# Attention into channel mix on one core: softmax weights turned by VectorE and DMAs in place of TensorE from the third batch on

## The chip, the cores and the metric

One core of a Trainium2 chip runs the whole program. The metric is the time of one execution in microseconds (us). The kernel before has a median of 829.65 us over 3 runs (829.41 to 830.24).

## The reference

q, k and v have 8 batches of 8 heads, 576 positions and 64 dimensions; s has one number for each head and position. Everything is float32. The output of the attention, with the heads side by side, is the input x of the second half.

```
scores = q @ k.T / 8                           # per batch and head, 576 x 576
cum    = cumsum(max(s, 0))
scores = where(key > query, -1e9, scores + min(-(cum[query] - cum[key]), 0))
attn   = exp(scores - rowmax);  attn = attn / (rowsum + 1e-9)
x      = attn @ v                              # (8, 576, 512)

xk = mu_k * x + (1 - mu_k) * x_prev            # x_prev: x one position earlier
xr = mu_r * x + (1 - mu_r) * x_prev
k  = max(xk @ w_k, 0)                          # 512 -> 1024
out = sigmoid(xr @ w_r) * ((k * k) @ w_v)      # 1024 -> 512
```

## The kernel before

**Visits and chunks.** A visit is one batch and one pair of heads. The first batch is visited in two parts for each pair (8 short visits), the other seven batches whole (28 visits), so there are 36 visits. The channel mix goes over 18 chunks of 256 tokens; a batch has 2.25 of them. A chunk can start once all four visits of its batch have stored their output to x_d in DRAM.

**One head of a whole visit.** The queries lie in five tiles t = 0 to 4 of 64, 128, 128, 128 and 128 rows, the keys in five blocks kb of 128, 128, 128, 128 and 64. `products` (L816) makes the scores of a query tile against all keys up to its end, as two matmuls in TensorE's reduced fp32 form (high and low halves); VectorE takes them out of PSUM with the row's minimum (L833); ScalarE exponentiates in place (L851); GpSimd divides by the row sum (L868, `normalize`). The result W has queries on partitions. The product with v needs keys on partitions. `weighted` therefore turns W by matmuls against an identity: 10 blocks of 128x128 (L933, `turn`) and 2 that hold two 64-column remainders together (L948, `turn_half`) for each head; ScalarE copies the turned blocks from PSUM to `ph` in seven pieces (L974, L991, L1003). So that two remainders lie side by side, VectorE writes the last 64 columns of tiles 2 and 4 in front of the rest (`lead`), in an instruction of its own, and tile 0's normalized weights go behind tile 1's. `both_heads` (L907) then makes the product with v for both heads at once, each head in its own 64 columns of the array, with full fp32 matmuls (each recorded as two instructions): per visit six products of 128, 448, 448, 320, 192 and 64 columns, 1600 in all. ScalarE copies the sums to xT (L1044), a DMA stores xT (L1350).

**Inputs.** For visits after the first batch a DMA brings k and q (raw, L747), GpSimd splits them in two (L769, L773), and four SBUF to SBUF DMAs of 64 partitions and 288 KB each place the halves (L782).

**Order.** All instructions are tasks of a planner (`Plan`). It puts them in a fixed order for each engine by a list schedule with written-out costs, due times and 40 passes forward and back; the order with the shortest planned time is emitted. Each engine, and the SP queue that issues nearly all DMAs, then works in that order and waits where a task isn't ready. The planner's costs for the new steps: a VectorE turn n/0.96 + 68 ns for n columns, a DMA 520 ns of the queue and 1300 ns more until it has landed.

Of the kernel before, what the change touches and what calls it, by code (L numbers as in the profile page):

```python
# [12 lines left out]
F32 = mybir.dt.float32  # L13
# [324 lines left out]
def forgetting_attention_then_channel_mix(  # L338
# [46 lines left out]
    def fixed(t):  # L385
        b = Buffer(lambda: t)
        b.ap = t
        return b
# [106 lines left out]


    NH = col(NQ - 1, P * (NQ - 1)) + 64
    phs = [fixed(const.tile([P, NH], F32, name=f"ph{j}")) for j in range(2)]

    def zero(t):  # L500
        for kb in range(NQ):
# [36 lines left out]
        )  # L538

    def constant_rows():  # L540
        for x in KLs + G2s:
            pool(lambda x=x: nc.gpsimd.memset(f32(x.get()[64:P]), 0.0), [], [(x, 1)], 2 * S, 36)
        for x in G2s:
            pool(
                lambda x=x: nc.gpsimd.memset(f32(x.get()[64 : 64 + PIECES]), 1.0), [], [(x, 1)], 2 * S, 36
            )
# [203 lines left out]
    def split_qk(x, b, hp):  # L750

        n = S
        KH = sbuf([P, 2, n], "KH", 2, F32R)
        G = sbuf([P, 2, n], "G", 2, F32R)
        KL, G2 = KLs[turns[0] % 2], G2s[turns[0] % 2]
        turns[0] += 1
        row = b * H + 2 * hp
        dma(
            lambda: nc.sync.dma_start(
                f32(KL.get()[64 : 64 + PIECES]), cum_d.ap[row : row + 2].rearrange("h p t -> p h t")  # L760
            ),
            [cum_d, (KL, 1)], [(KL, (j, 2)) for j in range(2)], 520,
        )

        def halves(r):
            return [(j, r) for j in range(2)]

        pool(
            lambda: nc.gpsimd.tensor_copy(KH.get(), x.get()),  # L769
            [(x, 0)], [(KH, p) for p in halves(0) + halves(1)], 2 * n, 114,  # L770
        )
        pool(
            lambda: nc.gpsimd.tensor_tensor(  # L773
                out=G.get(), in0=x.get(), in1=f32(KH.get()), op=ALU.subtract
            ),
            [(x, 0)] + [(KH, p) for p in halves(0) + halves(1)], [(G, p) for p in halves(0) + halves(1)],
            2 * n, 114, 2.21,
        )

        def move(to, a, y, c, r0, r1):  # L780
            dma(
                lambda: nc.sync.dma_start(f32(to.get()[a : a + 64]), f32(y.get()[c : c + 64])),  # L782
                [(y, p) for p in halves(r1)], [(to, p) for p in halves(r0)], 1370,
            )

        move(KL, 0, G, 0, 0, 0)
        move(G2, 0, KH, 64, 0, 1)
        move(G, 0, KH, 64, 0, 1)
        move(KH, 64, KH, 0, 1, 0)
        return G, G2, KH, KL  # L790

    def scores(b, h, tiles, G, G2, KH, KL):

        nm, sums, rinv = (sbuf([P, n], x, 2) for x, n in (("nm", 3 * NQ), ("sums", NQ), ("rinv", NQ)))
        if 0 in tiles:
# [4 lines left out]
        def products(t, m, i, k0, w, W):  # L800
            ps = bank(1, "s", 2)
            q0 = QS[t] - QS[tiles[0]]
            if G2 is None:
                pe(
                    lambda: nc.tensor.matmul(
                        ps.get()[:, :w],
                        G.get()[0:65, h % 2, q0 : q0 + P],
                        KH.get()[0:65, h % 2, k0 : k0 + w],
                        start=True,
                        stop=True,  # L810
                    ),
                    [(y, (h % 2, r)) for y in (G, KH) for r in range(2)], [ps], w, P, 4 / 2.4,
                )
            for x, (g, K) in enumerate(((G, KH), (G2, KL)) if G2 is not None else ()):
                pe(
                    lambda x=x, g=g, K=K: nc.tensor.matmul(  # L816
                        ps.get()[:m, :w],
                        g.get()[:, h % 2, q0 : q0 + m],
                        K.get()[:, h % 2, k0 : k0 + w],
                        start=x == 0,  # L820
                        stop=x == 1,
                    ),
                    [(g, (h % 2, 0)), (K, (h % 2, 0))]
                    + ([(g, 1), (K, (h % 2, 2))] if x else [(g, (h % 2, 1)), (K, (h % 2, 1))]), [ps], w, m,
                )

            n = KN[t]
            for a, e in ((k0, min(k0 + w, n - lead(t))), (max(k0, n - lead(t)), k0 + w)):
                if a >= e:
                    continue  # L830
                at = a + lead(t) if a < n - lead(t) else 0
                dve(
                    lambda a=a, e=e, at=at, i=i: nc.vector.tensor_tensor_reduce(  # L833
                        out=W.ap[:m, at : at + e - a],
                        in0=ps.get()[:m, a - k0 : e - k0],
                        in1=causal.get()[:m, S - P - QS[t] + a : S - P - QS[t] + e],
                        scale=-SCALE,
                        scalar=3.0e38 if i == 0 else nm.get()[:m, 3 * t + i - 1 : 3 * t + i],
                        op0=ALU.add,
                        op1=ALU.min,  # L840
                        accum_out=nm.get()[:m, 3 * t + i : 3 * t + i + 1],
                    ),
                    [ps, causal] + ([(nm, (t, i - 1))] if i else []),
                    [(W, i), (nm, (t, i))], e - a, ports="PS>S",
                )
                i += 1
            return i
# [12 lines left out]
            )  # L860

        def normalize(t, m, n, W):
            def to():
                u, a = pt[1].at
                return piece(u, a + P, 64, F32)[:64] if t == 0 else W.ap[:m, :n]

            pool(
                lambda: nc.gpsimd.tensor_scalar(  # L868
                    out=to(),
                    in0=W.ap[:m, :n],  # L870
                    scalar1=rinv.get()[:m, t : t + 1],
                    scalar2=1.0,
                    op0=ALU.mult,
                    op1=ALU.mult,
                ),
                [rinv] + [(pt[x], i) for x in (t, 1)[: 1 + (t == 0)] for i in range(3)],
                [(pt[1], 3)] if t == 0 else [(W, i) for i in range(3)], n, 244,
            )

        def rs(x):  # L880
            return x.get()[:, tiles[0] : tiles[-1] + 1]
# [13 lines left out]
        dve(lambda: nc.vector.reciprocal(rs(rinv), rs(rinv)), [], [rinv], 8 * len(tiles))  # L895
        for t in sorted(tiles, key=lambda t: t or 1.5):
            normalize(t, QN[t], KN[t], pt[t])
        return pt

    SWITCH = 95.0 + 54.0  # L900
# [19 lines left out]
        )  # L920
        plan.columns[i] = 4 * n

    def weighted(pts, V, xT, tiles):


        def transposed(pt, ph):
# [96 lines left out]
            if len(tiles) == NQ:  # L1023
                turned((0,))
                turned([(1, 2), (3, 4)], (2,))
                return turned((1,), (3,))
            elif tiles[0] == 0:
                turned((0,), [(1, 2)], (1,))
            else:
                turned((0, 2))  # L1030
                turned([(3, 4)], (2,), (3,))
        rest = [transposed(pt, ph) for pt, ph in zip(pts, phs)][1]
        po = bank(1, "po", 1)
        (*_, (q0, q1)) = spans = sums_of(tiles)
# [7 lines left out]
        for (a, e), ps in zip(spans, (rest, po)[-len(spans) :]):  # L1042
            act(
                lambda a=a, e=e, ps=ps: nc.scalar.copy(xT.get()[:, 1 + a : 1 + e], ps.get()[:, 0 : e - a]),  # L1044
                [ps], [(xT, a)], e - a, ports="P>S",
            )

    def sums_of(tiles):

# [226 lines left out]
    visits += [(b, hp, ALL) for b in range(1, B) for hp in range(NP)]  # L1276

    PLAIN = 8
    HEAD = 11200.0
    CHUNK = 40600.0  # L1280
    MARGIN = 25000.0
# [47 lines left out]
    prefix_sums()  # L1329
    plan.due = 25000.0  # L1330
    constant_rows()
    plan.due = 1000.0
    load_mu()
    for o in range(DF // 512):
# [7 lines left out]
    def finish(pts, V, xT, n, due):  # L1342
        b, hp, tiles = visits[n]
        plan.due = due
        weighted(pts, V, xT, tiles)
        q0, q1 = QS[tiles[0]], QS[tiles[-1]] + QN[tiles[-1]]

        c = slice(1 + q0 if q0 else 0, 1 + q1)
        dma(
            lambda: nc.sync.dma_start(x_d[b].ap[:, hp, c], xT.get()[:, c]),  # L1350
            [(xT, -1)] + [(xT, x) for x, _ in sums_of(tiles)],
            [(x_d[b], (hp, y)) for y in range(2) if tiles is ALL or y == (q0 > 0)],
            1300 * (q1 - q0) / S,
        )
        if hp == NP - 1:
            there[b] = q1

    for n, (b, hp, tiles) in enumerate(visits):
# [3 lines left out]
        if 0 < n < len(visits) - 1:  # L1362
            load(n + 1)
        plan.due = due
        xT = sbuf([P, S + 1], "xT", 2)
        pool(lambda xT=xT: nc.gpsimd.memset(xT.get()[:, 0:1], 0.0), [], [(xT, -1)], 2, 36)
        for j in range(2):
            plan.due = due + j * step
            pt = scores(b, 2 * hp + j, tiles, *QKs[n])
            if j == 0:  # L1370
                other = pt
            else:
                finish((other, pt), Vs[n], xT, n, due + (j + WDUE) * step)
            if j == 0 and n + 1 < len(visits):
                plan.due = due + SPLIT * step
                prepare(n + 1)
# [54 lines left out]
```

## Time and profile before

| | |
|---|---|
| median of 3 runs | 829.65 us |
| the profiled execution: its time, its span | 832.11 us, 830.3 us |
| TensorE busy, share of the span | 814.3 us, 98% |
| VectorE, ScalarE, GpSimd busy | 482.8, 558.5, 348.8 us |
| DMA moved | 104.9 MB, mean 126 GB/s |
| granted TensorE clock, mean | 0.99 |

Busy time is what the profile records as running; for TensorE it covers overlapping records, so a busy TensorE can still be waiting in parts. The span runs from the first to the last instruction; the 1.8 us beside it lie around the program.

### The profile page before, as it was taken

How to read it: one execution, taken by the hardware profiler on the slowest of the kernel's cores; microseconds unless marked ns; L12 is line 12 of the kernel's file. 1: busy time of each engine (PE TensorE's matmuls, PEld its weight loads, DVE VectorE, ACT ScalarE, POOL GpSimd, SP SyncE). 2: the span in 40 equal slices, each digit the busy share in tenths (PEclk: the TensorE clock that was granted, in tenths of full speed). 3: DMA queues.
4: the chain of work that ended last, by engine and by line, in shares of the span. 5: the costliest groups of instructions: out<-in, count | busy, mean ns of one | idle time of the engine just before them, and what ended most of it. 6: DMA issues, size and time to landing. Idle time of an engine off the chain costs nothing.

```text
span 830.3 us, 16178 instructions
## 1 busy us (share of the span) xinstructions
PE 814.3 (98%) x5498; PEld 686.1 (83%) x5498; DVE 482.8 (58%) x1628; ACT 558.5 (67%) x1641; POOL 348.8 (42%) x620
## 2 busy tenths in 40 slices
PE   8989899999999999999999999999999999999998
PEld 5568689788888879887988888888888787988997
DVE  6999858376455655475554645465645655436421
ACT  4887679687586866688585867577757767546421
POOL 8996876453444345343343433434443332100000
PEclk8999899999999999999999999999999999999999
DMA  7878658645544455444634453555354341012000
GB/s 220 254 243 260 156 158 207 170 126 143 138 121 124 117 142 114 132 128 127 168 103 118 110 157 99 136 134 153 95 131 115 97 119 37 28 47 64 14 26 25
DMA packets 47266, 104.90 MB, mean 126 GB/s; under 512 B 7518, under 2 KB 21092, under 8 KB 47184
## 3 DMA queue, kind: packets, MB, share of 16 engines
q1 hardware_dynamic: 47024, 103.71, 46.1%
q8 instruction: 43, 0.70, 0.4%
q14 instruction: 39, 0.32, 0.1%
q10 hardware_dynamic: 160, 0.16, 0.1%
HBM read 51.34 MB, written 19.48 MB: 85 GB/s over the span
## 4 chain that ended last, share of the span: by engine, by line
PE 77%; ACT 8%; POOL 5%; DVE 5%; DMA 3%; issue 2%; POOLq 0%; ACTq 0%
PE m L1220 19%; PE m L1148 17%; PE s L816 9%; PE m L1190 9%; PE po L907 8%; PE t L933 5%; ACT xp L1085 3%; DMA x<-x_d 3%; ACT W L851 2%; DVE xp L1096 2%; PE s L1220 2%; POOL W L868 2%; PE s L1148 1%; PE t L1148 1%; PE t L1220 1%
## 5 line engine op out<-in xcount | busy, mean ns | idle before, releaser
L851 ACT ACTIVATE W<-W,nm 128x448 f32<-128x448 f32 (+4 forms) x320 | 179.3, 562 | 73.0 <-DVE nm L833 66.1
L833 DVE CUSTOM_DVE_ANT_0 W<-s,causal 64x64 f32<-64x64 f32 (+4 forms) x320 | 129.2, 412 | 127.2 <-PE s L816 104.2
L1148 PE MATMUL m<-xh,w_k 128*128 128x256 f32 x1024 | 201.5, 285 | 0.0
L868 POOL TENSOR_SCALAR W<-W,rinv 128x448 f32<-128x448 f32 (+4 forms) x320 | 164.9, 536 | 19.7 <-DVE rinv L895 16.9
L1220 PE MATMUL m<-w_v,kh 128*128 128x512 f32 (+1 forms) x512 | 171.0, 394 | 0.0
L1148 PEld LDWEIGHTS m<-xh,w_k 128*128 128x128 f32 x1024 | 164.2, 189 | 1.4
L1148 PE MATMUL m<-xl,w_k 128*128 128x256 f32 x512 | 144.7, 283 | 0.0
L974 ACT COPY ph<-t 128x256 f32<-128x256 f32 (+3 forms) x264 | 102.1, 420 | 14.6 <-PE t L933 13.7
L1220 PEld LDWEIGHTS m<-w_v,kh 128*128 128x128 f32 x512 | 94.6, 188 | 15.2
L1096 DVE SCALAR_TENSOR_TENSOR xp<-x,mu,xp 128x256 f32<-128x256 f32 (+3 forms) x172 | 72.0, 419 | 51.6 <-ACT xp L1085 48.9
L1220 PE MATMUL m<-w_v,kl 128*128 128x512 f32 (+1 forms) x256 | 101.5, 397 | 0.0
L816 PE MATMUL s<-KH,G 128*64 128x64 f32 x336 | 97.3, 299 | 4.1 <-DVE nm L833 4.1
L890 POOL TENSOR_SCALAR rinv<-sums 128x5 f32<-128x5 f32 (+2 forms) x72 | 17.2, 240 | 194.5 <-ACT W L851 191.0
L1148 PEld LDWEIGHTS m<-xl,w_k 128*128 128x128 f32 x512 | 97.1, 190 | 0.8
L816 PE MATMUL s<-KL,G 128*64 128x64 f32 x336 | 97.0, 297 | 0.0
L907 PE MATMUL po<-ph,V 128*64 128x448 f32 (+4 forms) x688 | 94.5, 407 | 0.0
L1085 ACT ACTIVATE xp<-x,mu 128x256 f32<-128x256 f32 (+3 forms) x172 | 72.4, 421 | 29.1 <-DMA x<-x_d 9.6
L933 PE MATMUL t<-ident_r,Wr 128*128 128x128 f32 x640 | 87.9, 250 | 3.5 <-POOL W L868 2.4
L1190 PE MATMUL m<-w_r,xh 128*128 128x512 f32 x256 | 88.7, 403 | 0.9 <-DVE kl L1177 0.8
L933 PEld LDWEIGHTS t<-ident_r,Wr 128*128 128x128 f32 x640 | 68.7, 141 | 13.8 <-POOL W L868 5.8
L773 POOL TENSOR_TENSOR G<-raw,KH 128x1152 fp32r<-128x1152 f32 x28 | 74.9, 2676 | 1.9
L907 PEld LDWEIGHTS po<-ph,V 128*64 128x64 f32 x688 | 45.9, 139 | 33.1 <-issue 19.8
(130 smaller groups left out, 1356.9 us busy)
## 6 DMA issues: line engine op xcount, KB each, us to landing
raw<-in_q SPq DMA_DIRECT2D x28, 576.0 KB
G<-KH SPq DMA_DIRECT2D x56, 288.0 KB
V<-in_v SPq DMA_DIRECT2D x32, 320.0 KB
out<-g SPq DMA_DIRECT2D x35, 256.0 KB
x_d<-xT SPq DMA_DIRECT2D x28, 288.5 KB
KL<-G SPq DMA_DIRECT2D x28, 288.0 KB
KH<-KH SPq DMA_DIRECT2D x28, 288.0 KB
x<-x_d SPq DMA_DIRECT2D x12, 514.0 KB
```

The source lines that it names most:

```text
L816: lambda x=x, g=g, K=K: nc.tensor.matmul(ps.get()[:m, :w], g.get()[:, h % 2, q0 : q0 + m], K.get()[:, h % 2, k0 : k0 + w], start=x == 0, s ...
L833: lambda a=a, e=e, at=at, i=i: nc.vector.tensor_tensor_reduce(out=W.ap[:m, at : at + e - a], in0=ps.get()[:m, a - k0 : e - k0], in1=causal ...
L851: lambda: nc.scalar.activation(W.ap[:m, :n], W.ap[:m, :n], AF.Exp, bias=nm.get()[:m, 3 * t + mi : 3 * t + mi + 1], scale=-1.0, accum_out=s ...
L868: lambda: nc.gpsimd.tensor_scalar(out=to(), in0=W.ap[:m, :n], scalar1=rinv.get()[:m, t : t + 1], scalar2=1.0, op0=ALU.mult, op1=ALU.mult,),
L907: nc.tensor.matmul(po.get()[64 * j : 64 * j + 64, at : at + n], V.get()[:, kb, j], phs[j].get()[:, col(kb, a) : col(kb, a) + n], start=fir ...
L933: lambda: nc.tensor.transpose(ps.get()[0:m, place : place + P].bitcast(F32R), piece(pt[t].at[0], pt[t].at[1] + lead(t) + k0, m), ident_r.ap,),
L974: act(lambda: nc.scalar.copy(strips(ph), src()), [ps], [(ph, k) for k in ks], n * m, ports="P>S")
L1085: lambda n=n, o=o, i=i, to=to: nc.scalar.activation(to(), x.get()[:, c, o + i + 1 : o + i + 1 + n], AF.Copy, scale=mu.ap[:, which, c : c + 1],
L1096: lambda n=n, o=o, i=i, to=to: nc.vector.scalar_tensor_tensor(out=to(), in0=x.get()[:, c, o + i : o + i + n], scalar=mu1.ap[:, which, c : ...
L1148: lambda u=u, f=f, c=c, n=n, w=w, x=x: nc.tensor.matmul(ps.get()[:, u * CT : (u + 1) * CT], weight["k", c, f // 4].get()[:, w, f % 4 * P : ...
L1190: lambda c=c, n=n, x=x, w=w: nc.tensor.matmul(ps.get(), x.get()[:, c, ts], weight["r", c, 0].get()[:, w], start=c == 0 and n == 0, stop=c ...
L1220: lambda f=f, n=n, x=x, w=w, ps=ps, ms=ms: nc.tensor.matmul(ps.get()[:, :m], x.get()[:, f, ts], weight["v", f, 0].get()[:, w, ms], start=f ...
```

## The change

For visits 12 to 35 (`n >= BLOCKS`), which are batches 2 to 7, both heads' weights are turned otherwise. VectorE transposes W in blocks of 32x32 inside each group of 32 partitions and writes them to a new tile `turned` (`turn_blocks`): nine instructions for a head, with 64 to 512 columns, 1600 columns in all. When both heads are there, 16 DMAs move one quarter of the partitions each (32 partitions, 3840 bytes a partition) to a new tile `across`, which takes the place of both `ph` tiles; key group i of each DMA becomes a stretch of columns, so that keys lie on partitions. The product with v has nine products for a visit, of 64, 512, 64, 384, 64, 256, 64, 128 and 64 columns, again 1600. Visits 0 to 11 keep TensorE's transposes.

With it: `turned` and `across` have one buffer each; xT has one buffer in place of two, for all visits. Tiles 2 and 4 of the new visits are no longer written in two pieces (`first` is 0). Tile 0 is normalized in place. The second score matmul (`x` = 1) reads 67 partitions in place of 128, so that the four memsets of its unused rows and the wait on them go; four memsets (`blanks`) zero the parts of `turned` that no transpose writes. Planned costs, due times and steps are otherwise the same, and the planner orders everything anew.

```
...
+    ph_both = const.tile([P, 2 * NH], F32, name="ph")
+    phs = [fixed(ph_both[:, j * NH : (j + 1) * NH]) for j in range(2)]
+    NS = NQ * (NQ + 1)
+    turned_d = fixed(const.tile([P, 4, NS, 32], F32, name="turned"))
+    across = fixed(ph_both[:, 0 : 4 * NS * 32].rearrange("p (i s x) -> p i s x", i=4, s=NS))
+    across.last = phs
+    def slots(h, kb, t):
+        return (NQ + 1) * kb + t + 1 if h == 0 else (NQ + 1) * t + kb
+    def blanks():
...
-        for x in KLs + G2s:
-            pool(lambda x=x: nc.gpsimd.memset(f32(x.get()[64:P]), 0.0), [], [(x, 1)], 2 * S, 36)
...
-            [cum_d, (KL, 1)], [(KL, (j, 2)) for j in range(2)], 520,
+            [cum_d], [(KL, (j, 2)) for j in range(2)], 520,
...
-                        g.get()[:, h % 2, q0 : q0 + m],
-                        K.get()[:, h % 2, k0 : k0 + w],
+                        g.get()[: 64 + PIECES if x else P, h % 2, q0 : q0 + m],
+                        K.get()[: 64 + PIECES if x else P, h % 2, k0 : k0 + w],
...
-            n = KN[t]
+            n, first = KN[t], 0 if blocks else lead(t)
...
+        def turn_blocks(t, m, W):
+            j = h % 2
+            def at(a, e, g):
+                step = slots(j, 1, t) - slots(j, 0, t)
+                k0 = slots(j, a, t)
+                return turned_d.get()[:m, 0:g, k0 : k0 + step * (e - a - 1) + 1 : step].rearrange("p g k x -> p k g x")
+            for a, e, g in ((0, t, 4), (t, t + 1, 2)):
+                if a == e:
+                    continue
+                n = (e - a) * 32 * g
+                dve(
+                    lambda a=a, e=e, g=g, n=n: nc.vector.transpose(
+                        at(a, e, g),
+                        W.ap[:m, P * a : P * a + n].rearrange("p (k g x) -> p k g x", g=g, x=32),
+                    ),
+                    [(W, i) for i in range(3)], [(turned_d, (j, t))], n, ports="S>S",
+                )
...
+    def weighted_across(V, xT):
+        for g in range(4):
+            for i in range(4):
+                dma(
+                    lambda g=g, i=i: nc.sync.dma_start(
+                        across.get()[32 * g : 32 * g + 32, i], turned_d.get()[32 * i : 32 * i + 32, g]
+                    ),
+                    [(turned_d, (h, t)) for h in range(2) for t in range(NQ)], [(across, (g, i))], 520,
+                )
+        po, rest = bank(1, "po", 1), bank(1, "t", 2)
+        todo = [(rest, 0, 0, 0, 0, 2)]
+        for kb in range(NQ):
+            if kb:
+                todo.append((po, kb - 1, kb, kb, 2, 4))
+            if kb < NQ - 1:
+                todo.append((po, kb, kb, kb + 1, 0, 4))
...
+    BLOCKS = 12
...
-        xT = sbuf([P, S + 1], "xT", 2)
+        xT = sbuf([P, S + 1], "xT", 1)
```

## Rows read from the trace of the kernel before

**Rows 1.** The page: busy time by engine; the last chain, by engine.
```profile
PE 814.3 (98%) x5498; PEld 686.1 (83%) x5498; DVE 482.8 (58%) x1628; ACT 558.5 (67%) x1641; POOL 348.8 (42%) x620
...
PE 77%; ACT 8%; POOL 5%; DVE 5%; DMA 3%; issue 2%; POOLq 0%; ACTq 0%
```

**Rows 2.** SP's issues in time; L1350's issues after 190 us; start, duration.
```profile
194.28 0.83 SPq L1350 DMA_DIRECT2D x_d<-xT  x1
729.74 0.32 SPq L1350 DMA_DIRECT2D x_d<-xT  x1
...
L1350 SPq DMA_DIRECT2D x_d<-xT x24: 319/332/1164, 194.3 to 729.7; - x24
```

**Rows 3.** Busy time by stretch: stretch, length, engines, PEclk, DMA share, GB/s.
```profile
0.00:100.00 100.00, 90.06 (x563) 66.12 (x565) 89.34 (x273) 72.02 (x224) 83.29 (x150) 0.92 0.79 231
194.30:729.70 535.40, 532.46 (x3667) 453.19 (x3666) 293.97 (x1047) 374.41 (x1103) 207.87 (x373) 1.00 0.45 118
729.70:830.30 100.60, 97.50 (x587) 86.44 (x585) 40.92 (x76) 35.71 (x74) 0.00 (x0) 1.00 0.11 36
```

**Rows 4.** TensorE and its weight loads in time around eight transposes.
```profile
433.44 0.46 PE L933 MATMUL t<-ident_r,Wr 128*128 128x128 f32 x4
434.08 0.46 PE L1220 MATMUL m<-w_v,kh 128*128 128x512 f32 x1
...
433.21 0.55 PEld L933 LDWEIGHTS t<-ident_r,Wr 128*128 128x128 f32 x4
434.04 0.19 PEld L1220 LDWEIGHTS m<-w_v,kh 128*128 128x128 f32 x1
```

**Rows 5.** TensorE in time at one visit's product with v; L907 by form.
```profile
438.82 0.97 PE L907 MATMUL po<-ph,V 128*64 128x448 f32 x4
439.62 0.39 PE L907 MATMUL t<-ph,V 128*64 128x128 f32 x4
439.84 1.90 PE L907 MATMUL po<-ph,V 128*64 128x448 f32 x16
441.67 0.24 PE L816 MATMUL s<-KH,G 128*64 128x64 f32 x1
...
L907 PE MATMUL po<-ph,V 128*64 128x448 f32 x184 | 43.6, 552 | 0.0
L907 PE MATMUL po<-ph,V 128*64 128x64 f32 x92 | 6.5, 220 | 0.0
```

**Rows 6.** Four stretches around DMAs: columns as in rows 3.
```profile
401.80:403.30 1.50, 1.50 (x8) 1.21 (x7) 0.00 (x0) 0.00 (x0) 1.50 (x1) 1.00 0.87 184
427.75:429.25 1.50, 1.50 (x8) 1.20 (x7) 0.00 (x0) 1.46 (x7) 1.50 (x1) 1.00 0.87 189
430.50:435.20 4.70, 4.70 (x27) 3.98 (x26) 3.10 (x12) 4.64 (x16) 2.58 (x5) 1.00 0.94 250
```

**Rows 7.** L782's issues: ns least, median, most.
```profile
L782 SPq DMA_DIRECT2D KL<-G x28: 461/467/621, 69.6 to 665.8; - x28
```

**Rows 8.** VectorE groups by form: busy us, mean ns | idle before; two instructions in time.
```profile
L1119 DVE TENSOR_TENSOR xl<-xp,xh 128x512 fp32r<-128x512 f32 x64 | 44.0, 688 | 21.0 <-ACT xh L1115 20.7
L833 DVE CUSTOM_DVE_ANT_0 W<-s,causal,nm 128x64 f32<-128x64 f32 x128 | 35.7, 279 | 1.9
L833 DVE DVE_READ_ACCUMULATOR2_ANT nm<- 128x1 f32 x448 | 37.0, 83 | 0.0
...
430.44 0.32 DVE L833 CUSTOM_DVE_ANT_0 W<-s,causal 128x192 f32<-128x192 f32 x1
430.68 0.42 DVE L833 CUSTOM_DVE_ANT_0 W<-s,causal 128x256 f32<-128x256 f32 x1
```

**Rows 9.** ScalarE's copies of turned blocks, two of six forms.
```profile
L974 ACT COPY ph<-t 128x512 f32<-128x512 f32 x64 | 37.5, 586 | 7.4 <-PE t L933 7.2
L1003 ACT COPY ph<-t 64x128 f32<-64x128 f32 x112 | 29.5, 263 | 0.8
```

**Rows 10.** The last head's reciprocal; five normalizing instructions of one head.
```profile
715.54 0.19 DVE L895 RECIPROCAL rinv<-rinv 128x5 f32<-128x5 f32 x1 [0.59 <-POOL rinv L890]
...
439.85 2.57 POOL L868 TENSOR_SCALAR W<-W,rinv 128x192 f32<-128x192 f32 x5 [0.34 <-DVE rinv L895]
```

**Rows 11.** Waits: who for whom, us, times, longest.
```profile
POOL xT L1366 <- DMA x_d<-xT: 44.1, 10, 9.8
```

More of the change, by code (lines that the diff above doesn't have):

```diff
@@ L497, in forgetting_attention_then_channel_mix @@
     NH = col(NQ - 1, P * (NQ - 1)) + 64
-    phs = [fixed(const.tile([P, NH], F32, name=f"ph{j}")) for j in range(2)]
+    ph_both = const.tile([P, 2 * NH], F32, name="ph")
[7 more added lines that the diff above has]
+    def blanks():
+        u = turned_d.get()
+        for h in range(2):
+            a, step = slots(h, 0, 0), slots(h, 1, 1) - slots(h, 0, 0)
+            pool(
+                lambda a=a, step=step: nc.gpsimd.memset(
+                    u[:, 2:4, a : a + step * (NQ - 1) + 1 : step], 0.0
+                ),
+                [], [(turned_d, (h, t)) for t in range(NQ)], 64 * NQ, 36,
+            )
+            pool(
+                lambda a=a: nc.gpsimd.memset(u[64:P, 0:2, a : a + 1], 0.0), [], [(turned_d, (h, 0))], 64, 36,
+            )
     def zero(t):
@@ L790, in split_qk, with scores @@
         return G, G2, KH, KL
-    def scores(b, h, tiles, G, G2, KH, KL):
+    def scores(b, h, tiles, blocks, G, G2, KH, KL):
         nm, sums, rinv = (sbuf([P, n], x, 2) for x, n in (("nm", 3 * NQ), ("sums", NQ), ("rinv", NQ)))
@@ L825, in products @@
                 )
-            n = KN[t]
-            for a, e in ((k0, min(k0 + w, n - lead(t))), (max(k0, n - lead(t)), k0 + w)):
+            n, first = KN[t], 0 if blocks else lead(t)
+            for a, e in ((k0, min(k0 + w, n - first)), (max(k0, n - first), k0 + w)):
                 if a >= e:
                     continue
-                at = a + lead(t) if a < n - lead(t) else 0
+                at = a + first if a < n - first else 0
                 dve(
@@ L862, in normalize @@
         def normalize(t, m, n, W):
+            aside = t == 0 and not blocks
             def to():
                 u, a = pt[1].at
-                return piece(u, a + P, 64, F32)[:64] if t == 0 else W.ap[:m, :n]
+                return piece(u, a + P, 64, F32)[:64] if aside else W.ap[:m, :n]
             pool(
@@ L875, in normalize @@
                 ),
-                [rinv] + [(pt[x], i) for x in (t, 1)[: 1 + (t == 0)] for i in range(3)],
-                [(pt[1], 3)] if t == 0 else [(W, i) for i in range(3)], n, 244,
-            )
+                [rinv] + [(pt[x], i) for x in (t, 1)[: 1 + aside] for i in range(3)],
+                [(pt[1], 3)] if aside else [(W, i) for i in range(3)], n, 244,
+            )
+        def turn_blocks(t, m, W):
[14 more added lines that the diff above has]
+                    [(W, i) for i in range(3)], [(turned_d, (j, t))], n, ports="S>S",
+                )
         def rs(x):
@@ L897, in scores @@
             normalize(t, QN[t], KN[t], pt[t])
+            if blocks:
+                turn_blocks(t, QN[t], pt[t])
         return pt
@@ L921, in both_heads, with weighted @@
         plan.columns[i] = 4 * n
-    def weighted(pts, V, xT, tiles):
+    def weighted(pts, V, xT, tiles, blocks):
         def transposed(pt, ph):
@@ L1031, in transposed @@
                 turned([(3, 4)], (2,), (3,))
+        if blocks:
+            return weighted_across(V, xT)
         rest = [transposed(pt, ph) for pt, ph in zip(pts, phs)][1]
@@ L1046, in weighted, with columns, emit @@
             )
+    def weighted_across(V, xT):
[4 more added lines that the diff above has]
+                        across.get()[32 * g : 32 * g + 32, i], turned_d.get()[32 * i : 32 * i + 32, g]
+                    ),
+                    [(turned_d, (h, t)) for h in range(2) for t in range(NQ)], [(across, (g, i))], 520,
+                )
+        po, rest = bank(1, "po", 1), bank(1, "t", 2)
[5 more added lines that the diff above has]
+                todo.append((po, kb, kb, kb + 1, 0, 4))
+        def columns(h, kb, t, i, e):
+            n = 1 if e - i == 2 else NQ - t
+            step = slots(h, kb, 1) - slots(h, kb, 0)
+            a = slots(h, kb, t)
+            return across.get()[:, i:e, a : a + step * (n - 1) + 1 : step], n
+        def emit():
+            for ps, at, kb, t, i, e in todo:
+                for j in range(2):
+                    x, n = columns(j, kb, t, i, e)
+                    to = ps.get()[64 * j : 64 * j + 64]
+                    if ps is po:
+                        to = to.rearrange("p (i t x) -> p i t x", i=4, t=NQ - 1)[:, i:e, at : at + n]
+                    else:
+                        to = to[:, 0:64].rearrange("p (i t x) -> p i t x", i=2, t=1)
+                    nc.tensor.matmul(
+                        to, V.get()[:, kb, j], x,
+                        start=ps is rest or kb == 0, stop=ps is rest or kb == NQ - 1 or t == NQ - 1,
+                        skip_group_check=True,
+                    )
+        n = sum((e - i) * 32 * (1 if e - i == 2 else NQ - t) for _, _, _, t, i, e in todo)
+        k = plan.add(
+            "PE", SWITCH + 107.0 + n * 4 / 2.4, emit,
+            [V] + [(across, (g, i)) for g in range(4) for i in range(4)], [rest, po], land=54.0,
+        )
+        plan.columns[k] = 4 * n
+        act(
+            lambda: nc.scalar.copy(xT.get()[:, 1 : 1 + 64], rest.get()[:, 0:64]), [rest], [(xT, 0)], 64, ports="P>S",
+        )
+        act(
+            lambda: nc.scalar.copy(
+                xT.get()[:, 1 + 64 : 1 + S].rearrange("p (t i x) -> p i t x", t=NQ - 1, i=4),
+                po.get().rearrange("p (i t x) -> p i t x", i=4, t=NQ - 1),
+            ),
+            [po], [(xT, P)], S - 64, ports="P>S",
+        )
@@ L1331, in forgetting_attention_then_channel_mix @@
     constant_rows()
+    plan.due = 50000.0
+    blanks()
     plan.due = 1000.0
@@ L1344, in finish @@
         plan.due = due
-        weighted(pts, V, xT, tiles)
+        weighted(pts, V, xT, tiles, n >= BLOCKS)
         q0, q1 = QS[tiles[0]], QS[tiles[-1]] + QN[tiles[-1]]
@@ L1368, in forgetting_attention_then_channel_mix @@
             plan.due = due + j * step
-            pt = scores(b, 2 * hp + j, tiles, *QKs[n])
+            pt = scores(b, 2 * hp + j, tiles, n >= BLOCKS, *QKs[n])
             if j == 0:
```

## The prediction

> **What bounds the kernel now.** I read the page first, then the stretches, then single engines in time. In the page the reader is to see TensorE busy for 98% of the span, and a last chain that is TensorE for 77% [rows 1]. Busy is not the same as bound, so I looked at where the attention's pace comes from. The stores of xT mark the visits: the 24 that the change touches are stored from 194.28 to 729.74 us [rows 2]. That is 23 steps of 23.28 us. In the same stretch TensorE is busy for 532.5 of 535.4 us at full clock, VectorE for 294.0 (12.8 us a visit), and the DMA engines are 45% busy (10.5 us a visit) [rows 3]. So here TensorE sets the pace and the others have room. After the last store 100.6 us are left, with TensorE busy for 97.5 [rows 3]: three chunks, less work than which cannot follow the last store. So there are two clocks to watch: the sum of TensorE's work, and the time of the last store plus some 100 us.
>
> **What goes from TensorE.** 12 transposes a head, 48 heads: 576. Eight of them take 0.64 us from the first one's start to the next matmul's start, 0.83 us if counted between the weight loads [rows 4], that is 80 to 104 ns each. I take 90, nearer the matmuls' own starts: 24 in a visit are 2.16 us, 576 are 51.8 us (46 to 60).
>
> **What comes to TensorE.** The same 1600 columns, in nine products for six. The six take 2.85 us from 438.82 to 441.67 [rows 5]. A two-head product of 448 columns is busy 0.95 us (43.6 us over 46) and one of 64 is busy 0.283 us (6.5 over 23) [rows 5]: 1.73 ns a column and at most 0.17 us that doesn't go by columns, much of which overlaps the next product, as 1600 columns at 1.73 ns are already 2.77 of the 2.85 us. So a product more costs 0.013 to 0.17 us, three of them 0.04 to 0.5 us a visit. I take the low end, 1 us in all (12 at the other end), since the six together show it. The second score matmul streams the same columns over fewer partitions: nothing, as time goes by columns; TensorE's other work covers the rest.
>
> TensorE's need per visit thus falls from 23.28 to about 21.1 us. If nothing else changed the span would be 830.3 - 51.8 + 1 = 779.5 us.
>
> **What goes from ScalarE.** Seven copies a head, of 0.2 to 0.59 us [rows 9]. It is not the bound before and has more room after; I count no gain for it, and no cost.
>
> **What comes to VectorE.** Nine transposes a head with 1600 columns. No row shows a transpose there. The slope of its other instructions, between 512 columns in 688 ns and 64 in 279 [rows 8], is 0.91 ns a column; I use 1.04, the planner's rate, by which two neighbours, 192 columns and the next instruction 0.24 us later, leave 0.04 us of fixed cost [rows 8]. Low end: 1600 x 1.04 + 9 x 0.04 = 2.0 us a head. A lone instruction of 512 columns has 0.155 us beyond 1.04 a column, so with nothing overlapped it is 3.06. If a 4-byte block took two passes it would be 3.33 + 1.4 = 4.7, the upper end. I take 2.6, between the first two: the row nearest to it is a plain elementwise one. [...] Against the 5.2 us of a visit stand two merged pieces a head, each with an accumulator read of 83 ns and the fixed part of a 279 ns instruction [rows 8]: about 0.2 us each, 0.8 a visit. VectorE goes from 12.8 to 17.2 us a visit, 78% of a 22 us pace. It is not the bound, but it is in order, and its evacuation of scores and its part of the mix now stand behind transposes.
>
> **What comes to the DMA queue.** This is the term that I trust least. 16 transfers of 32 x 3840 bytes are 1.97 MB a visit, all on the one SP queue. The nearest row is one 64-partition move running alone: 184 to 189 GB/s at a share of 0.87 [rows 6], which is about 215 GB/s at a full share. 1.97 MB are 9.1 us at 215 and 10.4 us at 189. I take 9.7. The full rate of 16 engines is higher: with a 128-partition load among the moves the queue makes 250 GB/s [rows 6], by which it would be 7.9 us; but no transfer of the change has 128 partitions. [...]
> Issuing is no limit: 16 x 467 ns [rows 7] are 7.5 us, less than the 9.7. So the DMA engines have 10.5 + 9.7 = 20.2 us of work a visit. At TensorE's 21.1 us that would be a share of 0.96. The highest in the trace is 0.94, held for 4.7 us of transfers back to back [rows 6]; over 100 us it is 0.79 [rows 3], in a stretch that I can't show to be limited by DMA. The queue is in order: the 16 wait for the last VectorE transpose of the second head, and the k and q moves, the x loads and the stores queue behind. I take a share of 0.92, nearer the short row because the planner charges this queue for about what it costs. The pace is then 20.2/0.92 = 22.0 us.
>
> **What is later.** From the last head's reciprocal, 715.54, to its store, 729.74, pass 14.2 us now [rows 10, 2]. After: 2.6 us of normalizing [rows 10], about 1 of transposes still to come, 9.7 of transfers and about 2 to land, 2.9 of product, 1 of copy: 19. Five us more, once, at the last visit.
> One buffer for xT: GpSimd's memset now waits for the store of the visit just before. It waited 44.1 us in 10 waits with two buffers [rows 11]; GpSimd's room hides that (39% busy in the stretch [rows 3]); without it, up to 9.8 us once. The memsets that go and come are a few us of GpSimd outside the path.
>
> **The sum.** Span = 830.3 - 23 x (23.28 - 22.0) + 5 = 830.3 - 29.4 + 5 = 806 us. The profiled execution has 1.8 us around its span and lies 2.5 us above the median of the runs, so 805 in runs.
>
> **The rivals.**
> *TensorE stays the only bound.* For it: 99% busy, channel work that can fill any hole, and a share of 0.96 just possible. Against: three resources at 96, 100 and 81% of one pace. 779.5 to 785 us of span (with the 5 us hidden or not), some 781 in runs.
> *The DMA queue holds less.* Place: the SP queue in visits 12 to 35. At a share of 0.85 the pace is 23.8 us and the span 830.3 + 11 + 5 = 846; the point of decision is a pace of 23.06, a share of 0.876. For it: the long row's 0.79. Against: the queue is idle more than half the time now, and its waits before are on work of others.
> *VectorE takes two passes.* At 4.7 us a head VectorE has 12.8 + 9.4 - 0.8 = 21.4 us a visit; at 94% that is a pace of 22.8, a span of 824, and with it the small gain or none.
>
> **How the numbers follow.** DMA queue takes part of the gain (788 to 826): 0.46. TensorE only (776 to 788): 0.27. Less DMA share, slower (from 832): 0.18. VectorE in two passes or a mixture near no change (822 to 832): 0.09, half of it within 0.2%, which is about what a measurement of this kernel can tell from none (1.7 us). Faster 0.77, same 0.05, slower 0.18. The likeliest is 805, its own range 788 to 826. The range for 8 in 10 goes from 777, the clean TensorE sum, to 840, a share of 0.86; beyond lie 0.03 and 0.1.
>
> **What would show it.** TensorE's transposes 768 to 192 and some 52 us less of its time. VectorE's transposes: 432 instructions, 125 us in all; 225 would be two passes. A DMA share of 0.9 or more in the stretch of the 24 stores, at a pace of 22 us. A group of 16 transfers landing 10 to 12 us after its first issue. If the share stays under 0.85 while TensorE waits for `across`, the order and not the rate is the limit; if the pace is 21.1 at any share, the queue was no limit and I was wrong to give half of the gain back.

## The result, and the profile after

The changed kernel has a median of 798.04 us over 4 runs (793.36 to 801.71), the kernel before 829.94 (829.41 to 831.3). The ratio is 0.961, with a 95% interval of 0.9556 to 0.9665: 32 us faster. Its four runs differ by 1%, those of the kernel before by 0.2% (by up to 0.9% in the thirteen runs of it that lie beside each experiment). The order of the four is that of TensorE's mean granted clock: 0.994, 0.991, 0.991 and 0.985 from the fastest to the slowest. The profiled execution is the fastest of the four: 793.36 us, span 791.5, while the profiled execution before was 2.2 us above its median. Ratios here and below leave out runs over 1.5% above the fastest of the same kernel; medians are over all runs.

The page of the changed kernel: busy time by engine, the DMA queue (packets, MB, share of the 16 engines), and the chain that ended last; below it the DMA queue before.
```profile
PE 771.6 (97%) x5216; PEld 638.7 (81%) x5216; DVE 563.8 (71%) x1868; ACT 472.1 (60%) x1305; POOL 345.1 (44%) x620
...
q1 hardware_dynamic: 65456, 150.92, 73.4%
...
PE 56%; SPq 12%; DVE 11%; DMA 6%; POOL 6%; ACT 5%; issue 4%; DVEq 0%; ACTq 0%; POOLq 0%
```
```profile
q1 hardware_dynamic: 47024, 103.71, 46.1%
```
Against [rows 1], TensorE is 43 us shorter and ScalarE 86, VectorE 81 longer. The DMA engines are busy for 581 us (73.4% of 791.5) where it was 383 (46.1% of 830.3): 8.3 us for each of the 24 visits. In the last chain TensorE falls from 77% to 56%, and the SP queue, which wasn't in it, has 12%, VectorE 11.

The stores of the 24 visits, and busy time in that stretch and after the last store; columns as in [rows 2, 3].
```profile
L1461 SPq DMA_DIRECT2D x_d<-xT x24: 319/344/791, 199.5 to 692.6; - x24
...
199.50:692.60 493.10, 486.80 (x3368) 407.41 (x3367) 363.17 (x1242) 285.52 (x767) 203.23 (x363) 1.00 0.85 214
...
692.60:791.50 98.90, 95.84 (x579) 85.07 (x578) 40.80 (x76) 35.63 (x74) 0.00 (x0) 1.00 0.11 37
```
23 steps in 493.1 us are a pace of 21.44 us, where it was 23.28. The rest after the last store is as before (98.9 for 100.6 us), so the two profiled executions differ by the pace and by when the stores begin (199.5 for 194.3). TensorE is busy for 98.7% of the stretch, DMA for 85% (45% before).

One visit's product with v on TensorE in time, to be laid beside [rows 5].
```profile
429.88 0.34 PE L1133 MATMUL t<-ph,V 128*64 128x64 f32 x4
430.05 2.79 PE L1133 MATMUL po<-ph,V 128*64 128x512 f32 x32
432.76 0.38 PE L1256 MATMUL m<-xh,w_k 128*128 128x256 f32 x1
```
Nine products take 2.88 us; the six took 2.85.

VectorE's transposes: the group, and four of its six forms.
```profile
L920 DVE STREAM_TRANSPOSE turned<-W 128x64 f32<-128x64 f32 (+5 forms) x432 | 121.8, 327 | 28.8 <-DMA ph<-turned 11.7 <-POOL W L893 6.4 <-POOL rinv L937 3.2
...
L920 DVE STREAM_TRANSPOSE turned<-W 128x64 f32<-128x64 f32 x192 | 35.5, 202 | 0.0
L920 DVE STREAM_TRANSPOSE turned<-W 128x512 f32<-128x512 f32 x48 | 32.5, 678 | 0.1
L920 DVE STREAM_TRANSPOSE turned<-W 128x384 f32<-128x384 f32 x48 | 25.9, 539 | 0.2
L920 DVE STREAM_TRANSPOSE turned<-W 128x128 f32<-128x128 f32 x48 | 14.6, 304 | 27.7 <-DMA ph<-turned 11.7 <-POOL W L893 6.4 <-POOL rinv L937 3.2
```
2.54 us a head (121.8 over 48), 1.06 ns a column between the forms of 64 and 512. The wait of 11.7 us for `ph<-turned` (the page's name for a transfer from `turned` to `across`) is the one buffer of `turned`: the next visit's first transpose must wait for the 16 transfers. After these 8 waits VectorE went on 11.9 to 14.6 us behind the group's first issue.

The 16 transfers: the issues' duration in ns, one group in the queue's order of time, and the stretch of that group.
```profile
L1104 SPq DMA_DIRECT2D ph<-turned x384: 507/589/2127, 165.7 to 686.1; - x192
...
413.90 10.71 SPq L1104 DMA_DIRECT2D ph<-turned  x16
...
413.90:424.60 10.70, 10.70 (x51) 8.68 (x52) 7.96 (x25) 7.16 (x21) 2.90 (x7) 1.00 0.77 185
```
An issue holds SP for 0.589 us, not for the 0.467 of a 64-partition move [rows 7]. The group occupies SP for 10.7 us, and the DMA engines meanwhile have a share of 0.77.

The last head's reciprocal and its store, and GpSimd's waits for the one xT buffer.
```profile
672.21 0.19 DVE L942 RECIPROCAL rinv<-rinv 128x5 f32<-128x5 f32 x1
...
692.62 0.33 SPq L1461 DMA_DIRECT2D x_d<-xT  x1
...
POOL xT L1477 <- DMA x_d<-xT: 47.6, 16, 6.7
```
20.4 us, where it was 14.2 [rows 2, 10]; the wait for xT hardly differs from [rows 11].

### The profile page after: what moved, and what is told of

It is laid out like the page before. It is cut to its first block, busy times and chain, and to the rows that moved or that the text cites. A ratio compares the mean times of both kernels' runs of the same rounds, so it can differ in the third digit from the quotient of the medians.

```text
span 791.5 us, 16205 instructions
## 1 busy us (share of the span) xinstructions
PE 771.6 (97%) x5216; PEld 638.7 (81%) x5216; DVE 563.8 (71%) x1868; ACT 472.1 (60%) x1305; POOL 345.1 (44%) x620
## 3 DMA queue, kind: packets, MB, share of 16 engines
q1 hardware_dynamic: 65456, 150.92, 73.4%
## 4 chain that ended last, share of the span: by engine, by line
PE 56%; SPq 12%; DVE 11%; DMA 6%; POOL 6%; ACT 5%; issue 4%; DVEq 0%; ACTq 0%; POOLq 0%
PE m L1256 16%; PE m L1328 12%; SPq L1104 11%; PE s L839 6%; PE po L1133 5%; PE m L1298 5%; DVE turned L920 3%; DMA ph<-turned 2%; POOL W L893 2%; DVE W L856 2%; PE po L956 2%; DVE xp L1204 2%; PE s L1328 2%; DMA x<-x_d 2%; ACT xp L1193 2%
## 5 line engine op out<-in xcount | busy, mean ns | idle before, releaser
L1256 PE MATMUL m<-xh,w_k 128*128 128x256 f32 x1024 | 198.8, 283 | 0.5 <-DVE g L1338 0.5
L893 POOL TENSOR_SCALAR W<-W,rinv 128x192 f32<-128x192 f32 (+4 forms) x320 | 164.5, 529 | 26.8 <-DVE rinv L942 25.2
L856 DVE CUSTOM_DVE_ANT_0 W<-s,causal 128x448 f32<-128x448 f32 (+5 forms) x320 | 130.4, 419 | 45.9 <-PE s L839 40.1
L920 DVE STREAM_TRANSPOSE turned<-W 128x64 f32<-128x64 f32 (+5 forms) x432 | 121.8, 327 | 28.8 <-DMA ph<-turned 11.7
L937 POOL TENSOR_SCALAR rinv<-sums 128x5 f32<-128x5 f32 (+2 forms) x72 | 17.2, 238 | 199.6 <-ACT W L874 193.2
L839 PE MATMUL s<-KL,G 67*64 67x64 f32 x336 | 98.4, 296 | 0.0
L839 PEld LDWEIGHTS s<-KH,G 128*64 128x64 f32 x336 | 60.2, 180 | 20.6 <-DVE nm L856 15.0
L1133 PE MATMUL po<-ph,V 128*64 128x64 f32 (+4 forms) x768 | 67.1, 327 | 1.0 <-DMA KL<-cum_d 0.9
L839 PEld LDWEIGHTS s<-KL,G 67*64 67x64 f32 x336 | 60.2, 180 | 7.0
L1133 PEld LDWEIGHTS po<-ph,V 128*64 128x64 f32 x768 | 39.6, 137 | 26.8 <-issue 21.6
```

The source lines that it names most:

```text
L839: lambda x=x, g=g, K=K: nc.tensor.matmul(ps.get()[:m, :w], g.get()[: 64 + PIECES if x else P, h % 2, q0 : q0 + m], K.get()[: 64 + PIECES i ...
L893: lambda: nc.gpsimd.tensor_scalar(out=to(), in0=W.ap[:m, :n], scalar1=rinv.get()[:m, t : t + 1], scalar2=1.0, op0=ALU.mult, op1=ALU.mult,),
L920: lambda a=a, e=e, g=g, n=n: nc.vector.transpose(at(a, e, g), W.ap[:m, P * a : P * a + n].rearrange("p (k g x) -> p k g x", g=g, x=32),),
L1133: nc.tensor.matmul(to, V.get()[:, kb, j], x, start=ps is rest or kb == 0, stop=ps is rest or kb == NQ - 1 or t == NQ - 1, skip_group_check ...
L1256: lambda u=u, f=f, c=c, n=n, w=w, x=x: nc.tensor.matmul(ps.get()[:, u * CT : (u + 1) * CT], weight["k", c, f // 4].get()[:, w, f % 4 * P : ...
```

## Experiments

All are made from the changed kernel (median 798.0). In `half_dma`, `pe_more`, `more_dma`, `more_aside`, `dve_twice` and `act_half` the order of all instructions stays, as the planner doesn't see the edit; in the others it plans anew, so that they change the order as well. Ratios are to the kernel before, with 95% intervals.

**Is TensorE the bound, and what is missing?** By the prediction's sum TensorE alone would give about 779 us in runs; 798 was measured, so some 17 to 19 us are missing.

`half_dma`:
```
-  across.get()[32 * g : 32 * g + 32, i], turned_d.get()[32 * i : 32 * i + 32, g]
+  across.get()[32 * g : 32 * g + 32, i, 0:e], turned_d.get()[32 * i : 32 * i + 32, g, 0:e]   # e = 30, then 15
```


> Leaves out half of the columns of every transfer from the second visit of the new path on (the number of transfers and the order of all instructions stay), so the product with v works on old weights. Theory of the prediction (the DMA queue takes what TensorE gave up and the kernel didn't get: 798 measured against about 781 for TensorE's sum): the transfers cost 4.8 us a visit less, the 17 us come back, 780 to 787 us. Rival, TensorE is the only bound and the 17 us are its own: 795 to 799, nothing gained.


Measured: 785.51 us (784.98 to 793.83), ratio 0.9484 (0.9428 to 0.954), below the changed kernel's interval. `pe_more`:
```
+  for x in range(24):
+      nc.tensor.transpose(rest.get()[:, P * (x % 4) : P * (x % 4) + P].bitcast(F32R), ident_r.ap, ident_r.ap)
```


> Puts 24 transposes of the identity into TensorE before each visit's product with v (as many as the change removed; nothing waits for them and nothing is copied): 52 us of TensorE. If TensorE sets the pace now: 845 to 852 us. If the DMA queue or a wait sets it in part, they fill TensorE's idle time: 825 to 840.


Measured: 833.32 us (832.1 to 839.1), ratio 1.0058 (1.0031 to 1.0085). The stretch from 200 to 600 us of the changed kernel, of `half_dma` and of `pe_more`, in this order, columns as before.
```profile
200.00:600.00 400.00, 394.08 (x2722) 330.88 (x2721) 297.20 (x1026) 233.32 (x629) 172.12 (x303) 1.00 0.89 223
```
```profile
200.00:600.00 400.00, 399.08 (x2782) 338.50 (x2781) 305.09 (x1047) 240.83 (x650) 174.49 (x307) 1.00 0.68 181
```
```profile
200.00:600.00 400.00, 400.00 (x2980) 347.64 (x2980) 283.20 (x970) 224.05 (x602) 165.47 (x289) 1.00 0.84 209
```
The 24 stores of `half_dma` and of `pe_more`, and the added transposes of `pe_more`.
```profile
L1464 SPq DMA_DIRECT2D x_d<-xT x24: 319/336/783, 208.0 to 693.1; - x24
```
```profile
L1465 SPq DMA_DIRECT2D x_d<-xT x24: 319/345/786, 208.8 to 737.7; - x24
...
L1126 PE MATMUL t<-ident_r 128*128 128x128 f32 x576 | 52.6, 249 | 0.0
```
Both results lie where the prediction's theory had them. With half the bytes the median is 12.5 us lower, and TensorE is busy for 399 of 400 us: there it is, as far as the profile shows, the only bound. The pace is 21.09 us for 21.44, which is 8 us in the 23 steps, and the fastest runs of the two kernels differ by 8.4. (The profiled execution of `half_dma` is the longest of its four. Its stores begin 8 us later, and from 20 to 50 us its granted clock was 0.77, where the profiled execution of the changed kernel had 1.00; the new path starts behind that. Over the whole execution its clock was 0.981, that of the other three 0.991 to 0.993.) With 576 transposes put back (24 in each of 24 visits, busy for 52.6 us) the time rises by 35.3 us, so by this count 17 us of them filled time in which TensorE had been waiting. Busy records overlap: between `half_dma` and `pe_more`, in both of which TensorE is busy throughout, the pace differs by 1.90 us, 79 ns a transpose and 46 us in all, and by that 10 us were filled. TensorE thus still sets most of the time, and the transfers cost 8 to 17 us of what it gave up.

Where those go is seen in the waits between 200 and 600 us, of the changed kernel and then of `half_dma` (who for whom, us, times, longest).
```profile
DVE turned L920 <- DMA ph<-turned: 10.8, 7, 3.3
PEld s L839 <- DVE nm L856: 10.0, 17, 1.3
PE s L839 <- DVE nm L856: 3.5, 6, 0.8
PE t L1133 <- DMA ph<-turned: 0.6, 1, 0.6
```
```profile
DVE turned L920 <- DMA ph<-turned: 3.6, 3, 1.3
PEld s L839 <- DVE nm L856: 3.8, 9, 0.9
PE s L839 <- DVE nm L856: 0.8, 3, 0.5
```
TensorE hardly waits for `across` itself. Its score matmuls wait for VectorE, which must first empty the scores' place in PSUM, and VectorE in turn waits for `turned` to come free. With half the bytes both waits fall to about a third. That the one follows from the other is read from their falling together. In `half_dma` the group of 16 still holds SP for as long:
```profile
415.34 11.02 SPq L1107 DMA_DIRECT2D ph<-turned  x16
```
So the issues take as long with half the bytes (median 0.589 us in both), and what `half_dma` won hangs on the bytes, not on the issuing: issues, order and buffers are the same in both.

**How near the limit is the queue?** `more_dma`:
```
+  for _ in range(2 if i == 3 else 1)       # the transfer of i = 3 is sent twice
```


> Sends 4 of the 16 transfers of a visit twice, in the same place of the order: 2.4 us more of the DMA queue in each of 24 visits. If the queue sets the pace at the share that it holds now (0.85), the pace goes from 21.4 to 24.2 us and the time to 860. If TensorE alone sets it, 798 to 805. Between, about 820: the queue is near its limit but not at it.


Measured: 1031.97 us, ratio 1.2428 (1.2376 to 1.2481), far beyond every forecast. Who waited on the SP queue, longest first:
```profile
SPq L1105 <- DMA ph<-turned: 192.3, 96, 6.5
```
The second copy writes where the first has just written, so the program makes SP wait for each of the 96 until the first has landed, 2.0 us each on average. The edit was not the one I meant. `more_aside` sends the four to a tile of their own:
```
+  i == 3 and nc.sync.dma_start(spare_d[32 * g : 32 * g + 32], turned_d.get()[32 * i : 32 * i + 32, g, 0:15])
```


> Four more transfers a visit, of half the size (32 x 1920 bytes), from the tile of turned blocks to a tile that nobody reads, each behind every fourth of the 16; unlike the repeated transfers they write where nothing was just written, so the SP queue has no landing to wait for. They cost the engines 1.2 us and the SP queue's issuing 2.4 us a visit. If the time of the repeated transfers (1032) came from bytes and issuing: pace plus 1.2 to 2.4 us, 825 to 855. If it came from the four waits for a landing alone: 798 to 812.


Measured: 849.39 us, ratio 1.023 (1.0183 to 1.0277): 51 us more than the changed kernel, 2.1 us a visit, for 1.2 us of bytes and 2.4 of issuing. Of the 234 us of `more_dma`, some 183 are then the waits, which the trace sums to 192.3. In these two runs a microsecond that holds this queue costs about one of time, a fallen TensorE clock included (see the next experiment). `more_aside` doesn't move its bytes faster, but slower:
```profile
GB/s 224 256 253 224 259 132 206 189 214 199 217 221 191 208 210 222 214 223 203 201 201 214 230 211 195 216 233 225 219 210 205 189 171 165 136 72 52 26 26 25
...
DVE turned L921 <- DMA spare<-turned: 49.2, 16, 6.9
```
That is the rate by fortieths of the span and VectorE's wait for `turned`. No slice after the first five is above 233 GB/s, where the changed kernel's page has up to 246, and VectorE now waits 49.2 us in 16 waits for `turned` to come free. So a rate that is used up doesn't explain this run. The waits for `turned` point to a loop: the queue's time delays VectorE, and VectorE the rest.

**VectorE.** `dve_twice`:
```
-  nc.vector.transpose(at(a, e, g), ...)
+  [nc.vector.transpose(at(a, e, g), ...) for _ in range(2)]
```


> Does every transpose on VectorE twice, order unchanged: 5.1 us more of VectorE a visit, 15.8 to 20.9 us of a 21.4 us pace. If VectorE's place in the path takes part of the gain: 825 to 850. If it has room as busy shares say: 798 to 808.


Measured: 959.08 us, ratio 1.1555 (1.149 to 1.162). `dve_planned` is the same with the planner's cost raised from n to 2 n + 100 columns.


> Every transpose twice on VectorE as in the run before (959 us), but with twice the columns in the planner's cost, so that the order of all engines is made for it. VectorE then has about 22 us of work a visit. If 959 came from an order that didn't know of the work: 830 to 870. If VectorE's time itself is on the loop that sets the pace: 900 to 960.


Measured: 889.82 us, ratio 1.0713 (1.0661 to 1.0764). The transposes in `dve_twice`, then in `dve_planned`:
```profile
L921 DVE STREAM_TRANSPOSE turned<-W 128x64 f32<-128x64 f32 (+5 forms) x864 | 275.8, 346 | 28.3 <-DMA ph<-turned 7.1 <-POOL W L893 2.9 <-DMA KL<-cum_d 2.4
```
```profile
L921 DVE STREAM_TRANSPOSE turned<-W 128x64 f32<-128x64 f32 (+5 forms) x864 | 270.1, 344 | 28.5 <-DMA ph<-turned 7.2 <-DMA KL<-cum_d 2.5 <-POOL KH L792 1.1
```
154 us more of VectorE's work cost 161 us; with an order that knew of it, 148 us more cost 92. So some 70 us go with the order, and the rest with VectorE's own time, on an engine that the changed kernel's profile shows 74% busy (297 of 400 us). The first lies beyond both of its forecasts, the second between its two.

Part of both costs is TensorE's clock. The stretch from 200 to 600 us and the page's TensorE, in `dve_twice` and then in `dve_planned`, and three pieces of `dve_twice`.
```profile
200.00:600.00 400.00, 336.69 (x2116) 283.70 (x2115) 318.66 (x1043) 184.00 (x493) 131.24 (x234) 0.89 0.68 173
...
PE 838.2 (87%) x5216; PEld 692.1 (72%) x5216; DVE 715.2 (74%) x2300; ACT 472.2 (49%) x1305; POOL 344.9 (36%) x620
```
```profile
200.00:600.00 400.00, 358.54 (x2324) 295.59 (x2324) 344.35 (x1147) 198.44 (x543) 146.42 (x259) 0.95 0.75 190
...
PE 804.2 (91%) x5206; PEld 660.2 (74%) x5206; DVE 707.6 (80%) x2300; ACT 466.1 (53%) x1305; POOL 345.2 (39%) x620
```
```profile
313.00:317.00 4.00, 3.89 (x44) 2.44 (x42) 3.79 (x14) 1.08 (x2) 2.56 (x5) 1.00 0.74 222
317.00:321.00 4.00, 0.00 (x0) 0.00 (x0) 3.86 (x10) 1.58 (x3) 0.00 (x0) 0.88 0.15 35
322.00:326.00 4.00, 4.00 (x20) 4.00 (x20) 3.29 (x13) 2.35 (x9) 0.00 (x0) 0.50 0.46 103
```
TensorE stood still from 317 to 321 us, and from 322 to 326 us it worked at a granted clock of 0.50. In the whole stretch its mean clock was 0.89, and 0.95 in `dve_planned`, where the changed kernel has 1.00. The same matmuls are busy for 838 and 804 us, where it was 772. So in these runs TensorE waits more and is slower besides; how much of the 161 and the 92 us the clock is was not separated, and that the waits bring the clock down is not shown. Between 200 and 600 us the clock is below 1.00 in `more_dma` (0.87; 0.895 over its whole execution), `more_aside` (0.97), `act_half` and `cost650` (0.98 each) too.

**Issuing from two queues.** `act_half`:
```
-  nc.sync.dma_start(...)
+  (nc.scalar if i >= 2 else nc.sync).dma_start(...)
```


> Issues 8 of the 16 transfers from ScalarE's queue, at the same place in the order. The same bytes on the same 16 engines; SP's queue has 8 issues of 0.59 us fewer to make in front of the moves and loads behind them. If bytes set the limit (theory of the prediction): 795 to 803, unchanged. If issuing in order on SP does: 782 to 790. ScalarE is held while it issues, 4.7 us a visit; if that is on the path: 810 to 840.


Measured: 843.98 us, ratio 1.0146 (1.0078 to 1.0213).
```profile
L1104 SPq DMA_DIRECT2D ph<-turned x192: 507/588/1654, 173.3 to 730.2; - x192
L1104 ACTq DMA_DIRECT2D ph<-turned x192: 514/515/1358, 175.6 to 733.5; - x192
```
SP was relieved of 192 issues; ScalarE was held for 0.515 us by each, about 99 us in all, and the kernel lost 46 us, more than the highest of its forecasts. So SP's share of the loop can't be had cheaply from ScalarE. Whether SP's issuing alone costs the 8 to 17 us stays open, as this run changes two things.

**The rest of the change.** `rest_only`: `BLOCKS = 36`.


> BLOCKS = 36: no visit takes the new path; what is left is one buffer for xT, 67 partitions in the second score matmul, no memsets of its unused rows, the two ph tiles in one. I costed these at nothing: 827 to 833. Rival: xT's single buffer costs GpSimd waits, 833 to 845.


Measured: 828.33 us (826.94 to 834.3), ratio 0.9986 (0.9965 to 1.0007): nothing, as costed. All of the gain is the new path's, in the order that the planner made for it.

**Less, otherwise ordered, or fewer.** `trim` leaves the ten zero slots out of 8 of the 16 transfers; GpSimd clears their place once (not shown here):
```
...
+  def kept(x, g):
+      return x if g < 2 else x[:, 2:NS].rearrange("p (k s) x -> p k s x", s=7)[:, :, 0:5]
...
```


> The 8 transfers to the upper 64 partitions leave out the ten slots that are always zero (cleared once by GpSimd instead): 640-byte pieces, a third fewer bytes there, a sixth of all. Planned costs unchanged. The queue as the limit: 1 to 1.6 us a visit less, of which the 12.5 us that half the bytes gave bound the gain: 788 to 795. If short pieces cost more than they save: 798 to 815.


Measured: 806.14 us, ratio 0.9684 (0.963 to 0.9737). A sixth less bytes, in shorter pieces, brings nothing; its interval overlaps slightly with the changed kernel's, so that it is slower isn't certain, and the order is new as well. `alternate` only permutes the 16:
```
-  for g in range(4):
-      for i in range(4):
+  for r in range(4):
+      for x in range(4):
+          g, i = (0, 2, 1, 3)[x], (2, 0, 3, 1)[(x + r) % 4]
```


> Only the sequence of the 16 transfers is changed, so that source and target switch between the lower and the upper 64 partitions from one to the next. If two transfers on different halves can overlap, the group takes less than 10.7 us and the time is 783 to 792. If they follow one another at one rate whatever the partitions: 796 to 804.


Measured: 795.14 us (791.14 to 797.41), ratio 0.9572 (0.9524 to 0.962), within the changed kernel's interval and just between its two forecasts: alternating brings nothing that can be told from the spread. As half the bytes don't shorten a group either (11.02 us in `half_dma` for 10.71), this run can't show whether two halves overlap. `mix4`: one visit in four turns on TensorE again (`n >= BLOCKS and n % 4 != 3`).


> One visit in four of batches 2 to 7 goes back to TensorE's transposes: 18 visits on the new path. TensorE has 6 x 2.16 = 13 us more to do than in the changed kernel, the queue 2.7 us a visit less on the mean. If TensorE alone were the bound: 798 + 13 = 811. If the queue's group costs 17 us of the gain and a quarter less of it sets most of that free: 830 - 39 = 791, to 796.


Measured: 802.7 us, ratio 0.969 (0.9634 to 0.9747), between the two forecasts: of the 13 us that TensorE took back by the prediction's price, the queue's relief and the new order repaid about 8. `cost650` changes one number, the planned 520 ns of a transfer to 650.


> The planner charges each of the 16 transfers 650 ns of the queue in place of 520, about what the trace shows (16 in 10.7 us); the work is the same. If part of the 17 us is an order made for a queue that is too fast: 785 to 793. If not: 796 to 806.


Measured: 830.3 us (826.34 to 839.56), ratio 0.9991 (0.9971 to 1.0012), beyond both forecasts. The whole gain is gone with the same work. Its stores, GpSimd's waits for xT, and VectorE's for `turned`:
```profile
L1461 SPq DMA_DIRECT2D x_d<-xT x24: 326/390/1132, 216.5 to 728.9; - x24
...
POOL xT L1477 <- DMA x_d<-xT: 107.0, 12, 14.8
...
DVE turned L920 <- DMA ph<-turned: 1.8, 2, 1.0
```
The first of the 24 stores comes 17 us later and the pace is 22.28 us. GpSimd waits 107 us for xT's one buffer, where it waited 47.6. VectorE waits for `turned` only 1.8 us here, so this loss doesn't run over that buffer. That the waits for xT are the cause is not shown; that an order can cost the whole gain is. So the few us of `trim`, `alternate` and `mix4`, which were planned anew, may be the order's as well as the edit's.

No version tried beats the changed kernel beyond its interval with all of the computation.

## Why the prediction was right

It said 805 us in a range of 777 to 840, faster by a pace of 22.0 us because the DMA queue takes part of TensorE's gain. 798 us and 21.44 us (in the fastest of the runs) were measured. Time and direction came true, and that the transfers take part of the gain; but the sum that gave the pace came out near it by two errors that offset each other.

- **TensorE.** 51.8 us less for 576 transposes: confirmed from the other side, as the 576 put back are busy for 52.6 us and cost 46 us of the pace. Where the transfers are halved, the pace is 21.09 us for a need costed at about 21.1, and 785.5 us is what it leaves, 6 to 7 above the sum, with the last visit's 5 us in it. Three products more: 0.03 us a visit, costed at 0.04. The second score matmul on 67 partitions takes as long as before, 296 ns on average for 297, as costed.
- **ScalarE, and the rest of the change**, costed at nothing: `rest_only` agrees.
- **VectorE.** 2.54 us a head for 2.6. The rival with two passes had put it at 4.7, and falls. In the stretch VectorE is busy for 15.8 us a visit, not 17.2. But the price of its time was too low: the rival let it be busy for 94% of the pace, and by that rule the 5.6 us a head of `dve_planned` would be a pace of 24.7 us and about 868 us. 890 was measured, at a share of 0.86. The step that failed there is "it is not the bound", read from a busy share of 78%: the prediction names the order in which VectorE works, but puts no time to it. VectorE is inside the loop of transposes, transfers, moves and scores; added time there is paid.
- **The DMA term.** I had 9.7 us of engine time and "issuing is no limit" at 467 ns. The transfers cost the engines 8.3 us a visit, nearer the 7.9 that I had set aside. Issues of 32 partitions take 589 ns, the group 10.7 us on SP, at a share of 0.77. So issuing was the longer of the two, not the shorter, and where VectorE waited for a group it went on 11.9 to 14.6 us after the first issue, for 10 to 12 predicted. The sum of the stretch is a share of 0.85 at 21.44 us, 18.2 us a visit, for 20.2 predicted.
- **The share of 0.92.** This was the mechanism of the sum, and it is right in direction only: the kernel lost 8 to 17 us to the transfers (I gave 26), and at a share of 0.85 to 0.89. With the measured 8.3 us the same rule gives (10.5 + 8.3)/0.92 = 20.4 us, less than TensorE's own 21.1, and so no loss at all. That 22.0 us came out near 21.44 is luck: too much engine time, divided by too high a share. `more_aside`, `act_half` and `cost650` are slower at a share no higher. What the traces of the changed kernel and of `half_dma` show in its place is a chain of waits: the bytes hold `turned`, VectorE waits for it, and TensorE's scores wait for VectorE. The sign that I had set, TensorE waiting for `across`, didn't come (0.9 us in all).
- **The last visit.** 5 us more, measured 6.2. The 2 us to land in that sum stood on no row; the 96 waits for a landing in `more_dma` were 2.0 us each on average.

What stays open: how much of the 8 to 17 us each link of that chain has, and what SP's issuing and the order add to it. That the one buffer of `turned` is the link that counts is argued from its waits; a second buffer (15 KB a partition) wasn't tried.

## What to carry to other kernels

Work can be moved off a full engine onto a queue and a half-idle engine, but price what it moves onto by its loop and not by its busy share: here 52 us given up by TensorE became 32, and each further microsecond on the SP queue or VectorE came back as about 0.6 to 1, a fallen TensorE clock included. Count the issues of a DMA pattern, with the issuing time of their own shape, beside their bytes. Where a planner makes the order, rerun with slightly other costs before the gain is put down to the edit: one constant moved this kernel by 32 us.

## What was not expected of the hardware

An issue of 32 partitions between SBUF tiles holds SP for 0.589 us, one of 64 for 0.467 [rows 7], and halving the bytes doesn't shorten it (0.589 us in `half_dma` too). After standing still from 317 to 321 us, TensorE worked at a granted clock of 0.50 from 322 to 326 us (`dve_twice`). VectorE turns float32 in 32x32 blocks at the rate of a plain instruction, 678 ns for 512 columns beside 688 [rows 8].
